# Waits of an operation issued in the opposite order: the one expected last first

## The chip, the core and the metric

The kernel runs on one core of a Trainium2 chip, as one program. The core has engines that run side by side, each through its own queue of instructions: TensorE (PE; its weight loads are shown as PEld), VectorE (DVE), ScalarE (ACT), GpSimd (POOL) and SyncE (SP), which here issues nearly all DMAs. They know of each other only through semaphores: an instruction can raise one when it has finished, and an instruction, or a semaphore instruction ahead of it, can wait until one has reached a value. The metric is the device time of one execution, in microseconds.

## What is computed

A gated mix of two attention layers over one input x of 2048 rows and 512 columns, with 32 heads:

```python
g = _sigmoid((x * gate_w).sum(-1, keepdims=True))
a = _A_ref(x, A_mem0, A_Wq, A_Wk, A_Wv, A_Wo, A_seg_len)   # 64 segments of 32 rows
b = _B_ref(x, B_wq, B_wk, B_wv, B_wo, B_beta)              # 4 segments of 512 rows
return g * a + (1 - g) * b
```

Layer A is a recurrence over 64 segments. Each takes 8 rows of memory and 32 of x, projects them to q, k and v for 32 heads of 128, does masked softmax attention over the 40 rows, projects back, and its first 8 rows of output are the memory of the next segment:

```python
for s in range(n_seg):
    h = jnp.concatenate([mem, xs], axis=1)          # 40 rows
    q, k, v = (einsum('btd,dhe->bhte', h, W) for W in (Wq, Wk, Wv))
    p = _softmax(where(mask, einsum(q, k) * scale, -1e9))
    o = einsum(einsum(p, v), Wo)
    mem = o[:, :M, :].copy(); outs.append(o[:, M:, :])
```

Layer B has 4 segments of 512 rows, 32 heads of 16, causal softmax attention inside a segment and a running memory across segments.

## The kernel before

The kernel doesn't emit instructions as it goes. It records operations (`Prog.op`, `Prog.dma`), each with its engine, what it reads and writes, an expected cost and a function that emits its instructions: one for DVE, ACT and POOL as a rule, 4 to 64 matmuls for PE. From reads and writes it works out what each operation depends on (`_add`). `schedule` then places the operations with a model of their costs, and gives each an expected time of its end, `done`. The sequence on each engine is fixed by a table of numbers, `ORDER`, which `sequences` unpacks.

Layer A's segments set the pace: projections on PE (L1422), evictions by ACT and DVE (L1002), transposes on DVE (L1497), scores on PE (L1512, L1516) and their exponential on ACT (L1521), sums on PE (L1536) with logarithm and exponential on ACT (L1540, L1542), normalising on DVE (L1544) and POOL (L1546), the product with v on PE (L1577, L1586), the output projection (L1314), and the memory back into the next segment's input (L1332 to L1337). Pieces of layer B are placed between these: logits L1146, exponential L1164, mask on POOL L1170, product L1187, its evictions and normalising L1219 to L1244. L1345 and the DMAs L1357, L1613 and L1278 carry layer A's rows out, and L1289 mixes them with layer B's.

`emit` counts, for each engine, the operations that others depend on, and each of those raises its engine's semaphore by one when it ends (`sem_pe`, `sem_act`, `sem_dve`, `sem_gp`); DMA groups have semaphores of their own (`semg_...`). `waits` goes through all operations in the planned order and works out which semaphores each must wait for, and to what value; what is known through an earlier wait, directly or through another operation, is left out. The list `left` holds what remains, one entry for each engine or DMA group, sorted by the expected end of the operation waited for, a DMA's counted 1 us earlier. The body of each engine then calls `wait_ge` for each entry in that order (L547), and the operation's function after it. On POOL every operation also waits for the one before it.

Where an operation has one wait, it is carried by its first instruction. Where it has several, the built program has the wait that was emitted first on the instruction, and the others in semaphore instructions ahead of it.

Of the kernel before, what the change touches and what calls it, by code (L numbers as in the profile page):

```python
# [164 lines left out]
class Prog:  # L165
# [322 lines left out]
    def waits(self):  # L488

        known = {e: {} for e in self.ENGS}  # L490
        out = {}
        index = {id(o): (o.at, i) for e in self.ENGS for i, o in enumerate(self.ops[e])}
        for o in sorted(self.all, key=lambda o: index[id(o)]):
            have = known[o.eng]
            req = {}
            for d in o.deps:
                if isinstance(d, DmaOp):
                    key, val = d.group, 16 * (d.idx if d.group.ordered else d.group.count)
                else:
                    key, val = d.eng, d.seq  # L500
                if have.get(key, 0) < val and (key not in req or req[key][0] < val or req[key][1].done < d.done):
                    req[key] = (max(val, req[key][0]) if key in req else val, d)
            left = sorted(req.items(), key=lambda x: x[1][1].done - isinstance(x[1][1], DmaOp))
            for item in list(left):
                if any(x is not item and x[1][1].know.get(item[0], 0) >= item[1][0] for x in left):
                    left.remove(item)
            out[id(o)] = [(key, val) for key, (val, _) in left]
            for key, (val, d) in left:
                for k, v in d.know.items():
                    have[k] = max(have.get(k, 0), v)  # L510
                have[key] = max(have.get(key, 0), val)
            o.know = dict(have)
            if isinstance(o, DmaOp):
                if o.group.ordered:
                    o.know[o.group] = max(o.know.get(o.group, 0), 16 * o.idx)
            elif o.post:
                o.know[o.eng] = max(o.know.get(o.eng, 0), o.seq)
        return out
# [1129 lines left out]
```

## Time and profile before

| | |
|---|---|
| time, median of 3 runs | 825.21 us (824.72 to 827.68) |
| the profiled execution's own time | 824.12 us, span 822.2 us |
| PE busy | 795.5 us (97%) |
| DVE, ACT, POOL busy | 642.5, 523.4, 259.7 us (78%, 64%, 32%) |
| granted TensorE clock | 0.999 |

The span is the time from the first to the last instruction in the trace; the execution's time is 1.9 us more. PE's busy time counts a matmul from its start to a modelled end, and matmuls overlap, so 97% doesn't say that PE can't do more. In the rows of the trace a number pair at the start is the start and the length in microseconds; "idle before <-releaser" says how long the engine had been idle and what ended the wait. Semaphore instructions aren't counted as busy.

### The profile page before, as it was taken

To read this page: it belongs to the slowest core of one execution; us is meant where nothing else is said; L and a number is where in the kernel's file an instruction comes from. 1 tells how busy PE (TensorE), PEld (TensorE's weight loads), DVE (VectorE), ACT (ScalarE), POOL (GpSimd) and SP (SyncE) were. 2 spreads that over 40 slices of the span, in tenths; PEclk is the share of its full clock that TensorE was granted. 3 is DMA by queue.
4 is the path that set the end of the run, shared out by engine and by line. 5 is a ranking of instruction groups with operands and counts; after the bars stand their busy time and mean duration, and the time that the engine had idled before them with its cause. 6 is when DMAs were issued, how large, how long until landed. Compare 5 with 4: busy or idle time off the path is not lost.

```text
span 822.2 us, 51771 instructions
## 1 busy us (share of the span) xinstructions
PE 795.5 (97%) x23607; PEld 506.2 (62%) x23607; DVE 642.5 (78%) x1681; ACT 523.4 (64%) x1198; POOL 259.7 (32%) x564
## 2 busy tenths in 40 slices
PE   9999999999999999999999999999999999999987
PEld 4456666656666566666656665656765666666655
DVE  4878888778879777777877887787876788787886
ACT  4666656776656656767667666577666656766662
POOL 4543221233223332422422322333323223332440
PEclk9999999999999999999999999999999999999999
DMA  9982202121210111121011111100111010010001
GB/s 337 414 243 58 51 9 43 35 51 27 47 25 21 45 27 39 32 46 33 16 37 47 37 24 44 30 24 19 40 47 29 22 30 22 16 25 22 22 21 36
DMA packets 71696, 45.14 MB, mean 55 GB/s; under 512 B 50046, under 2 KB 69942, under 8 KB 69942
## 3 DMA queue, kind: packets, MB, share of 16 engines
q1 hardware_dynamic: 70422, 40.92, 17.6%
q8 instruction: 185, 3.03, 1.6%
q10 hardware_dynamic: 1056, 0.92, 0.4%
q14 instruction: 33, 0.27, 0.1%
HBM read 30.33 MB, written 8.87 MB: 48 GB/s over the span
## 4 chain that ended last, share of the span: by engine, by line
PE 84%; DVE 7%; ACT 3%; DMA 2%; issue 2%; POOL 0%; SPq 0%; DVEq 0%; POOLq 0%
PE pb L1422 45%; PE pb L1314 17%; PE pb L1029 6%; PE pb L1146 4%; PE pb L1577 2%; PE pb L1187 2%; PE pb L1031 2%; PE pb L1512 2%; PE pb L1536 1%; PE pb L790 1%; DMA out_dram<-stg 1%; PE pb L1586 1%; DVE V_sb L1002 1%; PE pb L1235 1%; DVE OT_sb L1002 1%
## 5 line engine op out<-in xcount | busy, mean ns | idle before, releaser
L1164 ACT ACTIVATE PTB<-pb 128x640 bf16<-128x640 f32 x240 | 158.4, 704 | 41.8 <-PE pb L1146 30.5
L1002 ACT ACTIVATE st<-pb 128x512 bf16<-128x512 f32 (+2 forms) x232 | 113.1, 499 | 106.8 <-PE pb L1422 80.7
L1422 PE MATMUL pb<-Wv_sb,hT 128*32 128x512 bf16 x2048 | 153.4, 380 | 0.0
L1422 PE MATMUL pb<-Wq_sb,hT 128*32 128x256 bf16 (+1 forms) x3072 | 140.0, 308 | 0.5 <-DVE hT L1337 0.3
L1314 PE MATMUL pb<-Wo_sb,OT_sb 128*32 128x256 bf16 x4096 | 131.4, 273 | 5.1 <-issue 3.8
L1422 PE MATMUL pb<-Wk_sb,hT 128*32 128x512 bf16 x2048 | 132.3, 379 | 1.0 <-issue 0.6
L1314 PEld LDWEIGHTS pb<-Wo_sb,OT_sb 128*32 128x32 bf16 x4096 | 102.1, 96 | 16.1 <-issue 4.2
L1170 POOL TENSOR_SCALAR_AFFINE_SELECT PTB<-PTB 128x512 bf16<-128x512 bf16 x120 | 78.1, 651 | 90.9 <-ACT PTB L1164 84.3
L1422 PEld LDWEIGHTS pb<-Wq_sb,hT 128*32 128x32 bf16 x3072 | 80.9, 97 | 41.7 <-DVE hT L1337 3.8
L1546 POOL TENSOR_TENSOR PT_sb<-PT_sb,rc_sb 128x64 bf16<-128x64 bf16 x81 | 29.6, 365 | 188.4 <-ACT rc_sb L1542 179.3
L1422 PEld LDWEIGHTS pb<-Wk_sb,hT 128*32 128x32 bf16 x2048 | 54.6, 97 | 48.9 <-DVE ao L1345 2.2
L1002 ACT ACTIVATE OT_sb<-pb 128x320 bf16<-128x320 f32 (+1 forms) x139 | 57.4, 429 | 34.4 <-PE pb L1586 32.2
L1002 DVE CAST st<-pb 128x512 bf16<-128x512 f32 (+1 forms) x123 | 67.2, 549 | 15.4 <-PE pb L1422 12.8
L1002 DVE CAST OT_sb<-pb 128x320 bf16<-128x320 f32 (+2 forms) x121 | 56.5, 475 | 20.6 <-PE pb L1586 18.2
L1002 DVE CAST V_sb<-pb 128x512 bf16<-128x512 f32 x90 | 61.5, 683 | 9.9 <-PE pb L1422 8.8
L1497 DVE STREAM_TRANSPOSE QT_sb<-st 128x128 f32<-128x128 f32 (+1 forms) x192 | 61.8, 334 | 7.8 <-ACT st L1002 5.7
L1540 ACT ACTIVATE rc_sb<-pb 128x160 f32<-128x160 f32 x128 | 38.9, 304 | 43.8 <-PE pb L1536 37.0
L1332 DVE STREAM_TRANSPOSE pb<-pb 128x256 f32<-128x256 f32 x63 | 29.3, 465 | 42.4 <-PE pb L1314 42.2
L1422 PEld LDWEIGHTS pb<-Wv_sb,hT 128*32 128x32 bf16 x2048 | 49.5, 97 | 19.2 <-ACT st L1002 0.7
L1521 ACT ACTIVATE PT_sb<-pb 128x224 bf16<-128x224 f32 x128 | 45.5, 356 | 23.3 <-PE pb L1516 19.4
L1497 DVE STREAM_TRANSPOSE KT_sb<-st 128x256 f32<-128x256 f32 x128 | 54.5, 426 | 7.0 <-ACT st L1002 5.5
L1544 DVE TENSOR_TENSOR PT_sb<-PT_sb,rc_sb 128x160 bf16<-128x160 bf16 x128 | 44.2, 345 | 9.0 <-ACT rc_sb L1542 7.4
(200 smaller groups left out, 1461.3 us busy)
## 6 DMA issues: line engine op xcount, KB each, us to landing
Wv_sb<-in_A_Wv_dram SPq DMA_DIRECT2D x4, 1024.0 KB, 10.1
Wk_sb<-in_A_Wk_dram SPq DMA_DIRECT2D x4, 1024.0 KB, 20.5
Wq_sb<-in_A_Wq_dram SPq DMA_DIRECT2D x4, 1024.0 KB, 27.3
Wo_sb<-in_A_Wo_dram SPq DMA_DIRECT2D x4, 1024.0 KB, 20.7
rest_v<-stg SPq DMA_DIRECT2D x112, 32.0 KB
rem_v<-rest_v SPq DMA_DIRECT2D x28, 128.0 KB, 2.4
a_rows<-ao SPq DMA_DIRECT2D x63, 32.0 KB
stg<-a_rows SPq DMA_DIRECT2D x15, 128.0 KB
```

The source lines that it names most:

```text
L1002: self.P.op(("act", "dve"), (lambda a: a.activation(dst, src(), ACT.Copy), lambda d: d.tensor_copy(dst, src())), reads=reads, writes=write ...
L1029: ins = pe.matmul(out[32 * c:32 * c + 32], lhsT[:, 32 * c:32 * c + 32], rhs, start=start, stop=stop, tile_position=(0, 32 * c), **kw)
L1146: ins = pe.matmul(pb[slot.banks[i]][:, base + a - lo:base + b - lo], KT[r0:r1, 128 * kc:128 * kc + 128], Q[r0:r1, t0 + a:t0 + b], start=Tr ...
L1164: P.op("act", (lambda dst=dst, src=src: lambda a: a.activation(dst, src(), ACT.Exp, scale=0.25))(), reads=[pair], writes=["%s%d_%d" % (nam ...
L1170: P.op("gp", (lambda pt=pt, ii=ii: (lambda g: g.affine_select(pt, pt, ([[0, len(ii)]] if len(ii) > 1 else []) + [[1, 128]], ALU.is_ge, 0.0 ...
L1314: ins = pe.matmul(pb[so.b][p0:p0 + 32, 0:256], tok(r, g, l), half(h, d, q), start=(r == 0 and g == 0 and l < 2), stop=(r == 1 and g == 3 a ...
L1422: ins = pe.matmul(self.pb[sl.b][32 * g:32 * g + 32, 0:hi - lo], x[:, c, 0:32], cols, start=(c == 0), stop=(c == C - 1), tile_position=(0, ...
L1497: op("dve", (lambda dst=dst, src=src: lambda d: d.transpose(dst, src))(), reads=["st%d%s" % (i, tag)], writes=["%sT%d%s" % (kind, r, tag)] ...
L1521: op("act", lambda a: a.activation(PT[:, r, :], pb[rb.b][:, 0:224], ACT.Exp, scale=SCALE), reads=[rb], writes=["PT%d" % r, "PT%dr" % r], n ...
L1540: op("act", lambda a: a.activation(rc[:, r, :], pb[rb.b][:, 0:160], ACT.Ln), reads=[rb], writes=[rr], name="ln%d_%d" % (s, r), cost=t_act( ...
L1544: op("dve", lambda d: d.tensor_tensor(mine[r], mine[r], by_head(rc[:, r, :]), ALU.mult), reads=[rp, rr], writes=[rp], name="nrm%d_%d" % (s ...
L1546: op(("dve", "gp"), tuple((lambda e: e.tensor_tensor(rest[r], rest[r], late(rc[:, r, :]), ALU.mult)) for _ in range(2)), reads=[rp + "r", rr],
```

## The change

```diff
@@ -500,7 +500,7 @@
                 if have.get(key, 0) < val and (key not in req or req[key][0] < val or req[key][1].done < d.done):
                     req[key] = (max(val, req[key][0]) if key in req else val, d)
-            left = sorted(req.items(), key=lambda x: x[1][1].done - isinstance(x[1][1], DmaOp))
+            left = sorted(req.items(), key=lambda x: x[1][1].done - isinstance(x[1][1], DmaOp), reverse=True)
             for item in list(left):
                 if any(x is not item and x[1][1].know.get(item[0], 0) >= item[1][0] for x in left):
                     left.remove(item)
```

The list of waits of an operation is sorted the other way round, so `wait_ge` is called first for the wait that is expected to end last. No instruction comes or goes, no operation changes place, and each operation waits for the same semaphores and values as before. It touches the operations with two or more waits: 293 on PE, 242 on POOL, 103 on DVE, 47 on ACT, 13 on SP.

In the rows below the names in brackets are the semaphores that an operation waits for, in the order in which the built program has them; the last is on the instruction itself. First PE, near 813 us, where the sums of a segment (L1536) wait for ACT's exponential, and the product with v (L1577) for its operands:

```order
 L1029 MATMUL pb<-woB_sb,oT 32x512 x7
-L1536 MATMUL pb<-PT_sb,ones_sb 32x160 [waits sem_act,sem_dve]
+L1536 MATMUL pb<-PT_sb,ones_sb 32x160 [waits sem_dve,sem_act]
 L1536 MATMUL pb<-PT_sb,ones_sb 32x4x16
```

And a little further on, on PE too:

```order
 L1586 MATMUL pb<-PT_sb,rem_v 128x4x16 x3
-L1577 MATMUL pb<-PT_sb,V_sb 128x40 [waits sem_dve,sem_act]
+L1577 MATMUL pb<-PT_sb,V_sb 128x40 [waits sem_act,sem_dve]
 L1577 MATMUL pb<-PT_sb,V_sb 128x40 x15
```

Before, L1536 had ACT's wait in a semaphore instruction and DVE's on the first weight load; now ACT's is on the weight load and DVE's ahead of it. L1577 swaps DVE's and ACT's in the same way.

The second place is also on PE, near 29 us: layer B's product (L1187), which waits for three engines.

```order
 L1029 MATMUL pb<-xT,Wo_sb 32x512 x7
-L1187 MATMUL pb<-oT,V_0 32x512 [waits sem_dve,sem_act,sem_gp]
+L1187 MATMUL pb<-oT,V_0 32x512 [waits sem_gp,sem_act,sem_dve]
 L1187 MATMUL pb<-oT,V_0 32x512
 L1187 MATMUL pb<-xT,V_0 32x512
```

POOL's wait was on the instruction; now DVE's is, and POOL's and ACT's stand ahead.

## The prediction

> **What bounds the kernel now.** I read the page first: the busy shares and the chain that ended last.
>
> ```profile
> span 822.2 us, 51771 instructions
> ...
> PE 795.5 (97%) x23607; PEld 506.2 (62%) x23607; DVE 642.5 (78%) x1681; ACT 523.4 (64%) x1198; POOL 259.7 (32%) x564
> ...
> PE 84%; DVE 7%; ACT 3%; DMA 2%; issue 2%; POOL 0%; SPq 0%; DVEq 0%; POOLq 0%
> ```
>
> PE carries 84% of the chain, and nearly all of that is matmuls that follow each other. The rest is handing over: PE stops for a result of ACT or DVE, and ACT or DVE stop for PE. A change of the order of waits moves no work; it can only touch these hand-overs. So the second view is the waits, for PE's weight loads, which come ahead of the matmuls and are what really waits (columns: total us, times, longest):
>
> ```profile
> PEld pb L1146 <- ACT PTB L1164: 9.6, 24, 0.4
> ...
> PEld pb L1536 <- ACT PT_sb L1521: 7.3, 30, 0.4
> ...
> PEld pb L1422 <- DVE hT L1337: 5.9, 18, 0.9
> ```
>
> There is no big wait. There are many of 0.2 to 0.4 us, so a fixed cost of some tens of nanoseconds in each is a visible part of them. The third view is the line that issues the waits, L547: every wait that is an instruction of its own, by engine.
>
> ```profile
> L547 PEldq EVENT_SEMAPHORE  x295: 51/51/143, 5.3 to 815.2; - x148
> L547 POOLq EVENT_SEMAPHORE  x242: 17/17/78, 2.7 to 802.2; - x121
> L547 DVEq EVENT_SEMAPHORE  x103: 21/21/21, 48.2 to 817.5; - x103
> L547 ACTq EVENT_SEMAPHORE  x47: 17/17/17, 70.1 to 807.6; - x47
> L547 SPq EVENT_SEMAPHORE  x13: 17/17/17, 124.1 to 813.3; - x13
> ```
>
> These 700 belong to the operations with two or more waits. Of each such operation one wait rides on the operation's own instruction, and the others stand ahead of it as semaphore instructions. The order shown above tells which is which: the wait that the source emits first is the one on the instruction (last in the brackets), those emitted later stand ahead. Before, waits are emitted by expected end, earliest first. So it is the wait expected **last** that stands in the separate instruction, and that is the one the hand-over usually runs through.
>
> **What a late wait costs in each of the two places.** I take the same hand-over, ACT's exponential (L1521) to the sums on PE (L1536), twice: once through a separate instruction, once on the weight load itself. In each pair of rows the first is the producer, the second the first weight load.
>
> ```profile
> 812.84 0.36 ACT L1521 ACTIVATE PT_sb<-pb 128x224 bf16<-128x224 f32 x1
> ...
> 813.31 0.15 PEld L1536 LDWEIGHTS pb<-PT_sb,ones_sb 128*32 128x32 bf16 x6 [0.22 <-DVE V_sb L1002]
> ...
> 811.63 0.36 ACT L1521 ACTIVATE PT_sb<-pb 128x224 bf16<-128x224 f32 x1 [2.21 <-PE pb L1516]
> ...
> 812.04 0.31 PEld L1536 LDWEIGHTS pb<-PT_sb,ones_sb 128*32 128x32 bf16 x8
> ```
>
> Separate: the producer ends at 813.20, the load starts at 813.31, 0.11 us later. On the instruction: 811.99 to 812.04, 0.05 us. To the nanosecond of the records it is 105 against 43 from the semaphore's update, so 0.062 us a time. Matching every semaphore instruction to its weight load, I find 113 on PE where the separate wait came last and the load followed the update by exactly that 105 ns. The first and the last of the 113:
>
> ```profile
> 7.84 0.41 DVE L922 COPY xT<-pb 128x512 bf16<-128x512 bf16 x1
> ...
> 8.37 0.13 PEld L1031 LDWEIGHTS pb<-xT,Wo_sb 128*128 128x128 bf16 x2 [0.30 <-issue]
> ...
> 814.94 0.22 DVE L1002 CAST OT_sb<-pb 128x64 bf16<-128x64 f32 x1
> ...
> 815.27 0.20 PEld L1577 LDWEIGHTS pb<-PT_sb,V_sb 32*128 32x128 bf16 x16 [1.03 <-ACT OT_sb L1002]
> ```
>
> 8.25 to 8.37 and 815.16 to 815.27: 0.12 and 0.11 us. The same comparison on the other three engines, separate wait first, own wait second, in each pair of rows. DVE (an eviction of L1586's product), ACT (an eviction behind DVE's L1345), POOL (behind its own instruction before):
>
> ```profile
> 601.02 0.20 PE L1586 MATMUL pb<-PT_sb,rem_v 32*128 32x64 bf16 x4
> ...
> 601.38 0.49 DVE L1002 CAST OT_sb<-pb 128x320 bf16<-128x320 f32 x1 [0.70 <-PE pb L1586]
> ...
> 814.16 0.19 PE L1586 MATMUL pb<-PT_sb,rem_v 32*128 32x64 bf16 x4
> ...
> 814.43 0.36 DVE L1002 CAST OT_sb<-pb 128x192 bf16<-128x192 f32 x1
> ```
> ```profile
> 128.01 0.42 DVE L1345 TENSOR_TENSOR ao<-pb,st 64x256 bf16<-64x256 f32 x1
> ...
> 128.52 0.39 ACT L1002 ACTIVATE st<-pb 128x256 bf16<-128x256 f32 x1 [0.28 <-PE pb L1422]
> ...
> 78.49 0.42 DVE L1345 TENSOR_TENSOR ao<-pb,st 64x256 bf16<-64x256 f32 x1
> ...
> 78.94 0.38 ACT L1002 ACTIVATE st<-pb 128x256 bf16<-128x256 f32 x1 [2.41 <-DVE ao L1345]
> ```
> ```profile
> 799.75 0.62 POOL L1221 TENSOR_TENSOR t_sb<-t_sb,rmem 128x256 f32<-128x256 f32 x1
> ...
> 800.51 0.34 POOL L1546 TENSOR_TENSOR PT_sb<-PT_sb,rc_sb 128x64 bf16<-128x64 bf16 x1
> ...
> 799.33 0.33 POOL L1219 TENSOR_SCALAR rmem<-rmem,gP_sb 128x16 f32<-128x16 f32 x1 [0.49 <-DVE rmem L1242]
> ```
>
> DVE: 0.16 against 0.08 us, so 0.08 less. ACT: 0.09 against 0.03, so 0.06 less. POOL: L1546 starts 0.14 us behind the end of L1221 (800.37 to 800.51), and L1221, with one wait, started 0.09 behind the end of L1219 (799.66 to 799.75): some 0.06 less.
>
> The rule that bears on this is in the Trainium skill, Perfetto Trace Analysis, "Per-instruction lifecycle": at a sequencer-only instruction the sequencer itself stands still until the wait ends and decodes the next one only then, while an engine's instruction is pushed into a wait queue and the sequencer goes on. The 0.11 against 0.05 us agree with it. By that rule the change would also free the sequencer to run ahead; the first rival below prices that from rows.
>
> **The sum.** The change removes and adds no instruction: 700 semaphore instructions stay, and the semaphores of each operation swap places. What it moves is where the late wait stands.
>
> PE, all of it: 113 x 0.062 = 7.0 us. DVE: 18 matched cases x 0.08 = 1.4 us. ACT: 24 x 0.06 = 1.4 us. POOL: 224 x 0.06 = 13 us, but POOL is busy for 32% and mostly waits for others, so most of this only lengthens a wait. Only what lies on the path counts. I walked the records back from the end, at each step to the release or to the predecessor that fixed the start, and met a separate late wait 40 times on PE, 11 on DVE, 16 on POOL, once on ACT: 40 x 0.062 + 11 x 0.08 + 16 x 0.06 + 0.06 = 2.5 + 0.9 + 1.0 + 0.1 = 4.5 us. That is the first-order gain. It is too much, since at each of these places another release stands close behind. Carrying the new offsets through all records of the trace (each instruction at the later of its predecessor plus the spacing measured, and its updates plus the offset above) leaves 2.1 us of it if a matmul whose wait goes takes the median spacing of its kind, and 2.6 us if it takes the shortest. PE alone gives 1.3 to 1.6, DVE alone 0.5 to 0.6, POOL alone 0.1 to 0.2, ACT and SP nothing.
>
> Against it stand the operations where the wait expected first really came last. One, at 29.26 us: PE's L1187 waits for DVE, ACT and POOL, with POOL's on the weight load, and POOL's L1170 was the last.
>
> ```profile
> 28.55 0.65 POOL L1170 TENSOR_SCALAR_AFFINE_SELECT oT<-oT 128x256 bf16<-128x256 bf16 x1
> ...
> 29.26 0.10 PEld L1187 LDWEIGHTS pb<-oT,V 128*32 128x32 bf16 x2 [1.04 <-POOL oT L1170]
> ```
>
> 29.20 to 29.26 is the short hand-over; with POOL's wait in front it becomes the long one. I count 6 such on PE, 1 on DVE, 2 on ACT, 10 on POOL. On PE that is 6 x 0.062 = 0.4 us lost at most, and the carried result has it in already.
>
> What stays at nothing: SP's 13, whose sequencer waits in either place; and the cost of the early wait's own instruction, 51 ns on PE, which is there before and after. It is hidden now behind the late wait, and afterwards behind the matmuls that are still running or behind the late wait of the weight load; if that cover is gone it costs 0.05 us at that place.
>
> I take 2.6 us: 824.12 - 2.6 = 821.5 for the profiled execution (span 822.2 and 1.9 around it). The profiled time is 1.1 below the median of 825.21, so the median becomes 822.6, 0.3% faster. That is within the 0.5% that a measurement of this kernel can tell from no change (4.1 us).
>
> **Rivals.** *The freed sequencer adds to it.* "issue" is 2% of the chain, 16 us in which PE waited for nothing that the profile shows. If PE's sequencer no longer stands in front of the late wait, it takes in the code behind it meanwhile. For it: at 113 places it stood still until the update, and the first weight load at 8.37 is itself put down to "issue". Against it: much of the chain's issue time is away from these places. With the whole first-order gain and a quarter of the issue time, 4.5 + 4 = 8.5 us, 816.7; with either alone about 4.5, 820.7. Middle 819. Chance 0.36.
>
> *The order is wrong.* The sort goes by the planner's expected ends. If what is expected last mostly isn't, the long hand-over is put where the short one stood. The point from which it decides is one half: more than half of the operations in which the order matters. The price is then up to the first-order sum with the other sign, 4.5 us, 829.7. Against it: 113 to 6 on PE, 24 to 2 on ACT, 18 to 1 on DVE. For it: starts shift, and a pair that is close can turn round. This is the case on the slower side, together with whatever a fixed schedule does when its margins move. Chance 0.09.
>
> *It changes nothing,* because the path goes round every one of these places, or because the built program comes out the same. The rows of the order exclude the second. The first gives 825.2; it lies inside the forecast's own range.
>
> **How the numbers follow.** Forecast 0.55 (gain between 0 and 4 us), freed sequencer 0.36, wrong order 0.09. Faster by over 0.5%: the second case, 0.36. Within: 0.55. Slower: 0.09. For 8 in 10 I leave out the far half of the freed sequencer below and nearly all of the wrong order above: 818.6 to 825.6.
>
> **What would show it.** Right: in the trace after, PE's first weight load behind L1521 starts 0.05 us after the end in most operations with two waits, DVE's 601.38 case 0.08 and POOL's 0.08; L1187 near 29 us starts 0.06 us later; the waits of the weight loads on ACT and DVE each lose a few tenths to 2 us in total. The sequencer rival shows in a chain whose issue share falls below 2%. The forecast is wrong if the offsets of 105 and 43 ns belong to the kind of operation and not to the place of its wait, since then the swap moves nothing, or if the late weight load, now waiting in the queue, keeps something else from being done ahead.

## The result, and the profile after

The changed kernel takes 816.2 us (median of 6 runs, 813.9 to 817.1) against 824.9 us: 0.989 of it, 95% interval 0.987 to 0.991. That is 8.7 us faster, and below the range of the prediction. A second measurement of the same program (e12) gives 816.2 against 822.8, 0.992 (0.989 to 0.994). By these two the change is worth 6.5 to 8.7 us.

The page of the changed kernel, the same parts as of before:

```profile
span 811.9 us, 51762 instructions
...
PE 788.2 (97%) x23598; PEld 501.2 (62%) x23607; DVE 643.7 (79%) x1681; ACT 523.1 (64%) x1198; POOL 257.8 (32%) x564
...
PE 84%; DVE 8%; DMA 3%; ACT 2%; issue 2%; SPq 1%; POOL 1%; DVEq 0%; POOLq 0%; ACTq 0%
```

The other engines are busy for nearly the same time, within 2 us; PE's busy time shrank by 7 us, and the gaps between its instructions by 3. A second trace of the kernel before (e5 below) has PE busy for 791.5 us, so a part of the 7 belongs to the execution and not to the change. Now the hand-overs that the prediction named. The same place on PE as before at 813.31 (L1536 behind ACT's L1521), the same eviction on DVE as before at 601.38, and the product L1187 near 29 us, in the changed kernel's timeline (start, length):

```profile
802.77 0.36 ACT L1521 ACTIVATE PT_sb<-pb 128x224 bf16<-128x224 f32 x1
...
803.17 0.09 PEld L1536 LDWEIGHTS pb<-PT_sb,ones_sb 128*32 128x32 bf16 x1 [0.15 <-ACT PT_sb L1521]
```
```profile
594.59 0.20 PE L1586 MATMUL pb<-PT_sb,rem_v 32*128 32x64 bf16 x4
...
594.88 0.49 DVE L1002 CAST OT_sb<-pb 128x320 bf16<-128x320 f32 x1 [0.63 <-PE pb L1586]
```
```profile
28.60 0.65 POOL L1170 TENSOR_SCALAR_AFFINE_SELECT oT<-oT 128x256 bf16<-128x256 bf16 x1
...
29.37 0.12 PEld L1187 LDWEIGHTS pb<-oT,V 128*32 128x32 bf16 x2 [1.17 <-DVE etmp L1092]
```

803.13 to 803.17 is 0.04 us where it was 0.11. DVE's eviction starts 0.09 behind the end of the product, where it was 0.16. POOL's L1546, at 790.56, starts 0.08 behind the end of L1221, where it was 0.14. L1187, where the wait expected first came last, went the other way: 29.25 to 29.37, 0.12 where it was 0.06. By the nanoseconds of the records, weight loads that start exactly one long hand-over (104 to 105 ns) behind a separate wait fell from 113 to 13. So the mechanism is the one that the prediction described; its size is not.

The waits of the weight loads, the rows shown of before and one of "issue":

```profile
PEld pb L1146 <- ACT PTB L1164: 9.3, 23, 0.5
PEld pb L1536 <- ACT PT_sb L1521: 9.3, 40, 0.4
...
PEld pb L1422 <- DVE hT L1337: 6.7, 20, 0.9
...
PEld pb L1422 <- issue: 4.9, 8, 1.2
```

In the kernel before the last row reads:

```profile
PEld pb L1422 <- issue: 6.6, 14, 1.4
```

The waits that carry a name add up to the same as before (93.8 and 93.9 us), and L1536's grew from 7.3 to 9.3 us; the prediction had expected the waits on ACT and DVE to lose a few tenths to 2 us. What shrank is "issue", from 33.8 to 24.2 us over all weight loads (29.6 and 24.5 in the second traces of the two kernels), though not in every row: L1146's went from 9.4 to 10.1. A part of it is a matter of names. Of 112 of the 113 loads behind a late separate wait, 21 stand under "issue" in the trace before, with 5.6 us; in the trace after, not one.

### The profile page after: what moved, and what is told of

Read it like the earlier page. It is cut to its first block, busy times and chain, and to the rows that moved or that the text cites. A ratio compares the mean times of both kernels' runs of the same rounds, so it can differ in the third digit from the quotient of the medians.

```text
span 811.9 us, 51762 instructions
## 1 busy us (share of the span) xinstructions
PE 788.2 (97%) x23598; PEld 501.2 (62%) x23607; DVE 643.7 (79%) x1681; ACT 523.1 (64%) x1198; POOL 257.8 (32%) x564
## 4 chain that ended last, share of the span: by engine, by line
PE 84%; DVE 8%; DMA 3%; ACT 2%; issue 2%; SPq 1%; POOL 1%; DVEq 0%; POOLq 0%; ACTq 0%
PE pb L1422 46%; PE pb L1314 18%; PE pb L1029 6%; PE pb L1146 3%; PE pb L1187 2%; PE pb L1577 2%; DMA st<-in_gate_w_dram 2%; PE pb L1512 2%; PE pb L1536 1%; PE pb L1031 1%; DVE V_sb L1002 1%; PE pb L1586 1%; DVE st L1002 1%; PE pb L1235 1%; DVE QT_sb L1497 1%
## 5 line engine op out<-in xcount | busy, mean ns | idle before, releaser
L1314 PE MATMUL pb<-Wo_sb,OT_sb 128*32 128x256 bf16 x4096 | 130.8, 273 | 2.2 <-issue 1.8
L1314 PEld LDWEIGHTS pb<-Wo_sb,OT_sb 128*32 128x32 bf16 x4096 | 102.3, 96 | 12.6 <-issue 2.3
L1546 POOL TENSOR_TENSOR PT_sb<-PT_sb,rc_sb 128x64 bf16<-128x64 bf16 x81 | 28.9, 356 | 188.9 <-ACT rc_sb L1542 174.9
L1521 ACT ACTIVATE PT_sb<-pb 128x224 bf16<-128x224 f32 x128 | 45.5, 356 | 23.0 <-PE pb L1516 19.1
```

What stands on the lines that cost most here:

```text
L1314: ins = pe.matmul(pb[so.b][p0:p0 + 32, 0:256], tok(r, g, l), half(h, d, q), start=(r == 0 and g == 0 and l < 2), stop=(r == 1 and g == 3 a ...
L1521: op("act", lambda a: a.activation(PT[:, r, :], pb[rb.b][:, 0:224], ACT.Exp, scale=SCALE), reads=[rb], writes=["PT%d" % r, "PT%dr" % r], n ...
L1546: op(("dve", "gp"), tuple((lambda e: e.tensor_tensor(rest[r], rest[r], late(rc[:, r, :]), ALU.mult)) for _ in range(2)), reads=[rp + "r", rr],
```

## The experiments

**One engine at a time.** e1 sorts the other way on PE alone, e2 on all engines but PE:

```diff
-            left = sorted(req.items(), key=lambda x: x[1][1].done - isinstance(x[1][1], DmaOp))
+            left = sorted(req.items(), key=lambda x: x[1][1].done - isinstance(x[1][1], DmaOp), reverse=o.eng == "pe")   # e1; e2: !=
```

> The waits of PE's 293 operations with several waits are emitted latest first, those of the other engines as before. If the gain is the shorter hand-over alone, PE has about 60% of it (1.3 to 1.6 of 2.1 to 2.6 us when the offsets are carried through the trace), so 5 us of the 8.7. If PE's freed sequencer is the larger part, PE alone gives 7 us or more, and the steps at the boundaries of PE's code blocks (every 256 instructions) fall as in the changed kernel, from 15 over 0.35 us to about 8.

> The waits of ACT, DVE, POOL and SP latest first, PE's as before. Hand-over alone: 40% of the gain, 3 to 3.5 us. Freed PE sequencer: 0.5 to 1 us, and the steps at PE's code boundaries stay as they are in the kernel before.

(Here and below, a difference from the kernel before is its ratio times that kernel's median, 823 us; between two experiments it is that of their medians.) e1: 817.5 against 823.4 us, 0.993 (0.991 to 0.995), 5.8 us faster. e2: 821.8, 0.998 (0.997 to 1.000), 1.4 us faster. The sum, 7.2, is the change within its spread. PE's part lies between the 5 us and the 7 us or more of the two theories, nearer to the first; the others' part is nearer to the second.

**By the distance to a code boundary.** PE's program has some 47,500 instructions: 23,607 weight loads, as many matmuls and 295 semaphore instructions. The page of the changed kernel counts 185 packets of instructions on queue 8, one for every 257 of these:

```profile
q8 instruction: 185, 3.03, 1.6%
```

That fits blocks of 256, and the long steps do gather at one place in every 256 instructions: of those over 0.6 us between weight loads, 18 of 37 in the first trace of before, and 80 of 96 in e7's below, fall on the same 32 of 256 positions. In the first trace of before PE stands still at some of these boundaries, here between two instructions of one operation that waits for nothing:

```profile
291.86 0.66 PE L1187 MATMUL pb<-PTB,V 128*32 128x512 bf16 x10
293.42 0.29 PE L1187 MATMUL pb<-PTB,V 128*32 128x256 bf16 x4 [0.91 <-issue]
```

In the changed kernel this stop is gone. Adding up, at each of the boundaries, by how much the largest step between neighbouring matmuls exceeds 0.25 us, the first trace of before has 8.5 us and that of after 5.1. (How many instructions around a boundary are counted is a choice that moves such sums by 1 to 3 us.) That suggested that a sequencer standing at a late wait shortly ahead of a boundary asks for the next block too late. e3 reverses only the 40 operations within 32 instructions of a boundary, e4 only the other 253:

```diff
+            if o.eng == "pe" and len(left) > 1:
+                if nth in NEAR:          # e4: not in
+                    left.reverse()
+                nth += 1
             out[id(o)] = [(key, val) for key, (val, _) in left]
```

> Latest first only in those 40 of PE's 293 operations with several waits whose semaphore instruction lies at most 32 instructions ahead of a boundary between code blocks. Hand-over alone: 40 of 293 of PE's part, 0.5 to 1 us faster. If the sequencer that stands ahead of a boundary delays the fetch of the next block: 3 to 5 us faster, and most of the steps of about 1 us at boundaries (at 171, 293, 617 us in the kernel before) are gone.

> Latest first in the other 253 of PE's operations with several waits, and those near a boundary as before. Hand-over alone: 4 to 5 us faster. Code fetch: 1.5 to 3 us faster, with the steps of about 1 us at boundaries still there.

e3: 822.8, 1.000 (0.998 to 1.001). e4: 818.0, 0.994 (0.992 to 0.996), 5.0 us faster. The operations near boundaries bring nothing that is clear of the noise: e3's interval, 1.5 us faster to 1.1 slower, excludes the 3 to 5 us of the fetch theory, but not the 0.5 to 1 of the hand-over. That theory of the boundaries fell, and most of its starting point with it, as the next run shows.

**The kernel before, once more,** for a second trace.

> The kernel before, unchanged, for a second trace. If the steps at the boundaries of PE's code blocks belong to the program, they add up to 8.5 us again (what is over 0.25 us at each). If they differ from run to run, they come to between 4 and 7 us, as in the four experiments so far, also in those that hardly changed the time.

```profile
span 816.9 us, 51762 instructions
```

The same program, 5.3 us shorter than in the trace that the prediction was made from; its profiled execution took 818.9 against a median of 821.9 here. Its boundary steps add up to 6.1 us. The four kernels e1 to e4 have 5.7, 5.7, 5.6 and 4.4, the changed kernel 5.1 and 5.8. So a good part of the 8.5 was that one execution's. Not all of it: the stop shown above is there in the second trace too, if shorter.

```profile
291.22 0.29 PE L1188 MATMUL pb<-PTB,V 128*32 128x256 bf16 x4 [0.58 <-issue]
```

(The lines of this file stand one lower.) But it is gone in e2's trace as well, which leaves PE's waits as they were. The stops at boundaries come and go with small shifts, and they don't explain the change.

**Is it the freed sequencer?** e6 has the late wait on the weight load, as e1, and puts a semaphore instruction with the same late wait behind the operation's first 8 matmuls (in shorter operations ahead of the last one: behind the 3rd or 7th as a rule). e9 is the same with a value long reached. e10 has the order of before with that additional instruction:

```diff
+    def matmul(self, *args, **kwargs):
+        if self.left == 0:                            # behind 8 matmuls
+            self.eng.wait_ge(self.sem, 1)             # on the next matmul
+            self.eng.wait_ge(self.sem, self.val)      # apart; e9: 1 for self.val
+        self.left -= 1
+        return self.eng.matmul(*args, **kwargs)
```

> PE's waits latest first as in e1, so the late wait is on the weight load; but behind the operation's first 8 matmuls (or its last but one) stands a semaphore instruction with the same late wait, so that PE's sequencer stops there until the update as it did before. If the shorter hand-over is the gain: 3.5 to 5.5 us faster than before, like e1. If it is the sequencer's freedom to run ahead: within 1.5 us of the kernel before.

> Instruction for instruction e6, but the semaphore instruction behind the first 8 matmuls waits for a value that is long reached, so PE's sequencer doesn't stop there; late waits on the weight load in both. If e6 is slow because of its 276 additional semaphore instructions (at the 21 ns each by which e8 exceeds e1: 5.8 us), and only because of them: as slow as e6, within 1.5 us. If the stop itself costs: 5 to 7 us faster than e6, so about level with the kernel before.

> The same number of instructions as e6 and e9. Order of waits as in the kernel before (late wait in the semaphore instruction ahead, long hand-over, sequencer stopped there), and the semaphore instruction behind the first 8 matmuls has nothing left to wait for. Against e6 only the place of the stop and with it the hand-over differ: if the 0.062 us of the hand-over count, 3 to 6 us slower than e6; if the stop of the sequencer is all, level with e6 within 1.5 us. Against e9 it shows the whole effect of the change on PE with this number of instructions: 5 to 7 us slower, as the kernel before against e1, if the parts add up.

e6: 829.4, 1.009 (1.006 to 1.012). e9: 831.5, 1.010 (1.007 to 1.013). e10: 838.6, 1.018 (1.015 to 1.021). The three have the same additional instructions, 292 in the trace and not the 276 of the expectations; e9's row for them:

```profile
L120 PEldq EVENT_SEMAPHORE  x292: 51/51/51, 9.3 to 823.0; - x146
```

e6 met neither of its two expectations: it is slower than the kernel before, because of the price of the additional instruction. The pairs are what counts. e6 and e9 show no difference clear of noise (0.8 us by the ratios, give or take 3.6). That doesn't decide on the freed sequencer, though, since e6's stop hardly ever stops anything. In e9 the additional instruction waits for nothing, so its start tells when PE's sequencer gets there. At 112 places with a late wait it starts ahead of the operation's first weight load in only 22, and at the median 17 ns behind it; in e6 the two numbers are the same. So even where nothing is in its way, the sequencer seldom gets past the first 3 to 8 matmuls of an operation before the late wait ends.

And e10 is 7.1 us slower than e9 with the same number of instructions (4.4 to 9.0 by the spread of the 6 runs of each): moving the late wait from the semaphore instruction to the weight load has that worth on PE. It is close to the full sum of 113 x 0.062 = 7.0 us; e10 against e6 gives 7.6, give or take 3.5, where 3 to 6 was expected.

The price of the additional instruction was expected to be 21 ns: e9 is 14.0 us slower than e1, 48 ns for each of 292, when the instruction itself lasts 51. The traces put only a part of it at the place itself: the steps to the load behind the 292 instructions add up to 16.1 us in e9 and 7.7 in e1, 29 ns each.

**Every late wait on PE apart, or every one on the instruction.** Operations with a single wait get a second one that is long satisfied:

```diff
+                    if ename == "pe" and len(todo) == 1 and isinstance(todo[0][0], str):
+                        todo.insert(0, (todo[0][0], 1))     # e7: the real one apart; e8: append, the real one on the instruction
```

> On PE each of the 1037 operations with a single wait for an engine gets a second wait that is long satisfied, and the real one is put in the semaphore instruction; those with several waits as before. So the long hand-over of 105 ns stands at some 400 places instead of 113, and there are 1037 more semaphore instructions. If the hand-overs count nearly in full (e1: 5.8 of 7.0 us): 15 to 20 us slower than e8. If only as the carried offsets said (1.3 to 1.6 of 7.0): 4 to 6 us slower than e8.

> The same instructions as e7, but each late wait on PE on the weight load and the satisfied or early one in the semaphore instruction ahead of it, with those of several waits as in e1. Against e1 it has 1037 more semaphore instructions on PE. If these are hidden: as e1, 5 to 6 us faster than before. If each costs its 51 ns where PE's queue is short: up to 15 us slower than e1.

e7: 902.1, 1.097 (1.093 to 1.101). e8: 839.8, 1.021 (1.017 to 1.025). The chains of e7 and of e8, in this order:

```profile
PE 85%; issue 7%; DVE 4%; DMA 2%; ACT 1%; SPq 1%; POOL 0%; DVEq 0%
```
```profile
PE 87%; DVE 7%; issue 3%; ACT 2%; DMA 0%; DVEq 0%; POOL 0%
```

The difference of 62 us is three times the larger of the two expectations. The largest waits of the weight loads at L1314 (L1319 in these files), in e7 and in e8:

```profile
PEld pb L1319 <- issue: 33.4, 37, 1.7
```
```profile
PEld pb L1319 <- issue: 15.0, 21, 1.5
```

37 stops of up to 1.7 us, released by nothing that the profile shows. Here the boundaries do matter: the steps there add up to 42.5 us in e7 and 12.4 in e8, 30 of the 62 (between 22 and 38, as fewer or more instructions around a boundary are counted). The rest, 32 (24 to 40), is of the size of the hand-overs: 378 weight loads start 104 to 105 ns behind a separate wait in e7 and 10 in e8, and 368 x 0.062 = 23 us. That a sequencer which stands at almost every hand-over comes too late for the next code block fits these traces; no run shows it by itself. e8 costs 22.3 us more than e1 for 1037 instructions, 21 ns each and beyond the 15 us that was expected at most; by the count above 6.7 of the 22.3 are steps at boundaries (12.4 against 5.7). So less than half of the 51 ns shows in the time.

**Fewer semaphore instructions on PE.** Since each of them has a price, e11 takes the changed kernel and puts early waits on a matmul at the end of the operation before, where by the plan they are over and don't depend on that operation:

```diff
+            if all(by[key].done < p.at - 0.2 and by[key].know.get("pe", 0) <= before for key, _ in extra):
+                early[id(o)] = extra       # waited for on the last matmuls of p, the operation before
+                after[id(p)] = id(o)
```

> The changed kernel, and where it is safe by the plan PE's early waits are moved from their own semaphore instruction to a matmul at the end of the operation before, so that 174 of PE's 297 semaphore instructions go. At 21 ns each as between e1 and e8: 3.6 us faster than the changed kernel. If the early waits' instructions are hidden in the changed kernel: level with it, and slower where an early wait isn't over yet.

> The changed kernel, unchanged, for a second trace and more times beside the kernel before: 0.989 to 0.992 of it. Steps at PE's code boundaries over 0.25 us: 5 to 6 us in total, as in its first trace (5.1); the kernel before had 8.5 and 6.1 in its two.

e11: 809.7, 0.984 of before (0.981 to 0.986), 6.5 us below the changed kernel's 816.2 on the same chip where 3.6 was expected: 38 ns for each of the 174 that are gone. Its boundary steps are 2.0 us, 3 to 4 less than the changed kernel's, so a good part of the 6.5 is not the instructions' own time. What is left on PE:

```profile
L583 PEldq EVENT_SEMAPHORE  x121: 51/51/690, 3.2 to 801.5; - x121
```

## Why the prediction was wrong, step by step

**The hand-over, right.** 0.05 us for a wait on the instruction against 0.11 for one apart on PE, and that the change swaps them, was read from four rows and holds after the change. So do DVE's (0.07 less where 0.08 was forecast), POOL's, and the exception at L1187, by 0.06 in the other direction. The order of the planner was right in nearly all cases; the rival of the wrong order fell.

**All of PE, 7.0 us: near what was measured, in part by luck.** The prediction had it as an upper bound. e10 against e9 gives 7.1 (4.4 to 9.0), e1 against before 5.8 (4.0 to 7.5 by its interval). But the traces don't show 0.062 us at each place and nothing else. At 112 of the 113 places the first load starts 55 ns sooner behind the load before it, and the second follows the first by 9 ns where it was 33 to 34; but the fifth, where there is one without a wait, comes 32 to 37 ns later behind the fourth than before. In sum the steps to the first and second load shrink by 6.1 and 2.7 us, and those to the next seven grow by 3.9. That leaves 5.0 us (4.9 to 5.2 in the four pairs of traces); the rest of the gain stands elsewhere.

**The carrying, wrong. This is the step that failed:** "It is too much, since at each of these places another release stands close behind", by which the 4.5 us on the path (4.4, if it is rounded only at the end) became 2.6, with 1.3 to 1.6 for PE alone. The 4.5 counted only places on one backward walk, 40 of 113 on PE. The carrying took all places, but it held each step between instructions without a wait as it was in one trace, and let the waits that come next take back half of the gain. The two traces of each kernel show what happened. The steps between PE's weight loads, each pair's difference in us, in the order first before to first after, first to second, second to first, second to second:

| steps ahead of | count | differences | mean |
|---|---|---|---|
| operations with several waits | 293 | -5.6, -4.9, -5.9, -5.2 | -5.4 |
| instructions with one wait | 1098 | 2.7, 0.9, 2.3, 0.5 | 1.6 |
| loads at code boundaries | 1132 | -4.1, -3.4, 0.5, 1.2 | -1.4 |
| all others | 21083 | -3.2, -1.3, -1.8, 0.1 | -1.6 |
| whole | | -10.2, -8.6, -4.9, -3.3 | -6.7 |

In the carried working PE's steps shrank by 5.0 us ahead of operations with several waits, and 2.5 came back at later waits. The first was nearly right. What came back is 1.6; and the steps without a wait, which the working put at nothing, shrank by 3.0. That is the larger part of the 4 us that the carrying missed, and the less certain one: over the four pairs it runs from 7.3 less to 1.3 more, and 1.4 of it stands at boundaries, where the pairs disagree and the first trace of before has most of it. Why these steps shrank stays open. That PE is the engine everything waits for in the end was on the page, 84% of the chain. In this kernel the sum over its late waits, 7.0, came nearer to the measured 5.8 to 7.1 than the walk's 2.5 or the carrying's 1.3 to 1.6.

**DVE, ACT and POOL.** Forecast 0.6 to 0.8, measured 1.4 (0.2 to 2.6) together with SP, so this forecast is not refuted. How it divides among the four wasn't tried.

**The profiled time.** The prediction said that the profiled execution lay 1.1 us below the median. In later measurements the medians of before were 822.8 to 823.4, so it lay about 1 us above them, and the second trace's 3 below its own median. The spans of the two traces differ by 5 us, twice the forecast effect.

**The freed sequencer** was the rival whose time came nearest (816.7 to 820.7 against 816.2), but part of it for a wrong reason: its first half, that the first-order 4.5 us aren't taken back, was nearer to the measured gain than the forecast's 2.6; its second, a quarter of the "issue" time for a sequencer that takes in the code behind, has no run for it. The sign that the prediction named, a chain whose issue share falls below 2%, didn't come: it is 2% in both pages. Over all loads "issue" did shrink, but 5.6 us of that, in the first traces, stood at loads behind a late separate wait, which carry other names now. What the sequencer gains is small: in e9 it seldom gets past the first 3 to 8 matmuls, and the trace of the change shows it in the second load, which is 24 to 25 ns closer to the first, but the fifth gives more than that back. The rule of the Trainium skill that was cited there (Perfetto Trace Analysis, "Per-instruction lifecycle"), that the sequencer stands still at its own instructions, agrees with e7's 42.5 us at boundaries; for this change it decided nothing beyond the hand-over itself.

**Left open.** Why the steps without a wait shrank, by 3.0 us in the mean of the pairs. Nor do these runs separate how much of the shorter hand-over is the semaphore instruction's own 51 ns, which now passes ahead of the late wait's end, and how much the way from the sequencer to the weight load.

## What to carry to other kernels

In this kernel a wait that stood in an instruction of its own cost 62 ns behind the release, some more than that instruction's 51. So put the wait that ends last on the instruction that needs it, and let the early ones stand ahead of it, where most of their time is hidden. On the engine that bounds, don't discount a fixed cost in its late hand-overs by one walk along the chain, nor by a carrying that holds all other steps as they are in one trace: here the full sum came nearer. Better still, have fewer such instructions there: early waits fit on instructions that wait for nothing, as e11 shows.

## What the hardware showed that was not expected

On PE a semaphore instruction lasts 51 ns, and its price by the times of whole kernels goes from 21 ns each (1037 ahead of weight loads, e8) over 38 (174 taken out, e11) to 48 (292 in the middle of operations, e9); steps at code boundaries are a part of the first two. The steps at PE's code boundaries don't grow with the number of these instructions alone, but with what they wait for: 2.0 us with 121 (e11), 4.4 to 8.5 with 295, 5.2 to 6.0 with 587 (e6, e9, e10), 12.4 with 1332 of early or long satisfied waits (e8), 42.5 with 1332 of which each has the late wait (e7). Only the last stands clear of the choice of how many instructions around a boundary are counted. And with the late wait on the weight load PE's sequencer doesn't run far ahead: behind 3 to 8 matmuls an instruction that waits for nothing started, at the median of 112 places, 17 ns after the first load (e9).
